# One load per chunk, an opening without holds, and five changes of order in a retention and feed-forward kernel

## The chip, the cores and the metric

The kernel runs on one core of a Trainium2 chip. The metric is the time of one execution on the device, in microseconds (us). Before the change three runs took 639.9, 640.38 and 642.58 us; the median is 640.38. The profiled run took 638.22 us, of which the profile covers a span of 636.4 us.

The engines are named as the profile names them: PE (TensorE matrix products), PEld (its weight loads), DVE (VectorE), ACT (ScalarE), POOL (GpSimd) and SP (SyncE, which issues all the transfers).

## The reference

Two blocks follow each other: a retention layer, computed as a recurrence over 768 tokens for 4 sequences of 8 heads, and a feed-forward block with an ELU on its 3072 tokens.

```python
batch, n_heads, seq, head_dim = (4, 8, 768, 64)
n_tokens, d_model, d_ff = (3072, 512, 2048)

gamma = 1.0 - 2.0 ** (-5.0 - np.arange(H, dtype=np.float32))
scale = 1.0 / np.sqrt(D)
for t in range(S):
    state = gamma[None, :, None, None] * state + np.einsum('bhd,bhe->bhde', k[:, :, t], v[:, :, t])
    y[:, :, t] = scale * np.einsum('bhd,bhde->bhe', q[:, :, t], state)
# x: (B,H,S,D) -> (B*S, H*D)
h = x @ w_in
g = np.where(h > 0.0, h, alpha * (np.exp(np.minimum(h, 0.0)) - 1.0))
return (g @ w_out).astype(np.float32)
```

All inputs of the retention are fp32; the two weight matrices arrive as fp64.

## The kernel before

**Tiling.** The 3072 tokens are cut into 24 chunks of 128, and four chunks make a token block of 512, so there are six blocks (numbered 0 to 5). A chunk has one row of 2048 fp32 numbers for each of the 128 partitions: q and k turned (the tile `qk`, columns 0 to 1023) and k and v plain (the tile `kvn`, columns 1024 to 2047). `load_one` (L106) loads one of the two tiles in a transfer of 512 KB, and `load` (L99) both. Retention within a chunk goes over half chunks of 64 tokens: `score_products` (L308) multiplies q and k, `scores` or `mask_pair` mask the result on DVE, `scale_v` (L281) multiplies v by the powers of gamma (DVE for chunks 0 and 1, POOL for the others), `state_products` (L338) and `state_sum` (L349) make the running states, and `within` (L395) and `across` (L405) add up y. Two small DVE copies called `seen` (L384, L432) stand between the first and the second half of `across`. The scaled y becomes x, the input of the feed-forward block, in the tiles `xb` and `xt`.

**Weights.** They come as 16 pieces of fp64 bits, 1 MB each (`load_piece_parts`, L134), into three staging tiles, and are turned into fp32 by ACT (`prepare`, L151: L168, L170, L172) and DVE (`decode`, L184: L194, L195, L198). At the end of its decoding a piece asks for the next load, since its staging tile is then free. Pieces 0 to 7 are w_in (`w_a`, `w_b`), pieces 8 to 15 are w_out (`w_s` as a first stop).

**Products.** Block 0 uses plain products for the first matrix (`plain_first`, L495) and seven products for four (Strassen's scheme) for the second. Later blocks use the scheme once or twice nested. Its combined weights are made by `combine_w_out`, `combine_w_in` and, on POOL, `combine_small` (L816: four differences and sums of 128x512 at L821, the result written to DRAM). From block 1 on the weights of the second matrix are read back from DRAM in pieces of 256 KB (`wq`) through a ring of 11 tiles (`fetch_small`, L797); the first 11 fetches stand behind the last `combine_small` write on SP.

**Order.** All of it is written out by hand: each engine executes its instructions in the order in which the code emits them, and generators interleave the parts. Four places matter for the change. (1) The opening, L257 to L267 and L1106 to L1167: transfers are issued in the order in which the code wants them, and some are held back by `hold` (L116), a one-element POOL copy from an earlier tile into the new one, so that the new transfer can be issued only after the earlier one has landed. (2) The loop at L1278, which computes the first product of block 1 with `sides` (making combined weights on DVE) and `smalls` (`combine_small` on POOL, for j = 3 after its third turn and j = 2 after its fourth). (3) `second_twice` (L935), the second matrix of a block in products j = 1, 2, 6, 7, 5, 3, 4, each again in seven small products; it yields at points where retention steps of the next block are put in (`VISITS`, L1313: five visits in block 1). In it `copy` (L961, ACT) and `add` (L966, DVE) take the results out of PSUM. (4) `first_end` (L921), which ends a quarter of the first matrix with its ELU (`elu`, L478: ACT L483 and L484, and a DVE instruction L487 that may wait in the list `later`) and, for C22, makes the differences T3 and T1 (L930, L931).

Of the kernel before, what the change touches and what calls it, by code (L numbers as in the profile page):

```python
# [9 lines left out]
FP32 = mybir.dt.float32  # L10
# [8 lines left out]
def kernel(  # L19
# [76 lines left out]
    chunks = [divmod(m, NCH) for m in range(NCHUNK)]  # L96
    raw = {}

    def load(m):  # L99

        if m >= NCHUNK:
            return
        for which in range(2):
            load_one(m, which)

    def load_one(m, which, behind=None):  # L106
        if which == 0:
            raw[m] = [ldpool.tile([P, 2, HP, C], FP32, name="qk", tag="qk"), None]
            t = raw[m][0].rearrange("p a h c -> p (a h c)")
        else:  # L110
            raw[m][1] = ldpool.tile([C, 2, H, D], FP32, name="kvn", tag="kvn")
            t = raw[m][1].rearrange("p a h c -> p (a h c)")
        hold(t, behind)
        nc.sync.dma_start(t, qkv[m, :, 1024 * which : 1024 * which + 1024])

    def hold(t, other):  # L116

# [136 lines left out]

    powers_of(slice(0, 2 * C))

    load(0)  # L257
    parts = load_piece_parts(2)
    next(parts)
    for which in range(2):  # L260
        load_one(1, which, raw[0][which][:, 0, 0])
    next(parts, None)
    pieces = lambda n: staged[n][:, :, 0].bitcast(FP32)
    load_piece(pieces(0))
    load(2)
    load(3)
    load_piece(pieces(1))  # L267

# [542 lines left out]

    W_IN = {2: w_a_[:, :, :, 1], 3: w_s_[:, :, 2]}

    def combine_small(j):  # L816

        t = stage.tile([P, 4, 4, P], FP32, name="wi", tag="stage")
        a11, a12, a21, a22 = (W_IN[j][:, 2 * r : 2 * r + 2, :, c, :] for r in range(2) for c in range(2))
        s1, s2, s3, s4 = (t[:, k].rearrange("p (n f) c -> p n f c", f=2) for k in range(4))  # L820
        tt = lambda o, x, y, op: nc.gpsimd.tensor_tensor(out=o, in0=x, in1=y, op=op)  # L821
        tt(s1, a21, a22, ALU.add)
        tt(s2, s1, a11, ALU.subtract)
        tt(s3, a11, a21, ALU.subtract)
        tt(s4, a12, s2, ALU.subtract)
        to_send.append((scratch3[j - 1], t.rearrange("p k f d -> p (k f d)")))
# [94 lines left out]
    def first_end(n, name, ps, x=None):  # L921

        g = gq[name][:, 2 * n : 2 * n + 2, :]
        nc.vector.tensor_tensor(out=g, in0=ps, in1=g if x is None else x, op=ALU.add)  # L924
        g = g.rearrange("p a b -> p (a b)")

        def combine():
            mine = lambda x: gq[x][:, 2 * n : 2 * n + 2, :].rearrange("p a b -> p (a b)")
            sub = lambda o, x, y: nc.vector.tensor_tensor(out=o, in0=x, in1=y, op=ALU.subtract)
            sub(mine("T3"), mine("C22"), mine("C12"))  # L930
            sub(mine("T1"), mine("C12"), mine("C11"))  # L931

        return lambda: elu(g, g, 3, combine if name == "C22" else None)

    def second_twice(tb, behind_last):  # L935
# [121 lines left out]
        for at, j in enumerate(ORDER2):  # L1057
            last = j == 4 and tb == NTB - 1
            cur = (inner_end if last else inner)(j)
            next(cur)  # L1060
            if j == 1:
                yield "tail"
            for _ in before:
                pass
            if j == 2:
                flush()
                next_input(2)
            if j == 5:
                next_input(6)
            if j == 1:  # L1070

                next(cur)
                yield "elu"
                next(cur)
            parts = input_parts(ORDER2[at + 1]) if at + 1 < 7 else iter(())
            if j in (2, 5):

                next(parts)
            else:
                for _ in parts:  # L1080
                    pass
            if at == 6:
                behind_last()
            if j != 1:
                next(cur)
                yield "middle"
                next(cur)
            for _ in parts:
                pass
            before = cur  # L1090
            yield j
# [28 lines left out]
    y = outputs_of_first()  # L1120
    next(y)
    next(y)
    score_products(sc, 0, 0, 1)
    state_sum(kvs, 0, 0, 0, 1)
    prepare(2, between=lambda: powers_of(slice(2 * C, S)))
    piece = decode(True)
    take()
    take()
    mask_pair(sc, 1)
    scale_v(1)  # L1130
    unread(1, TB)
    inner = plain_first()
    next(inner)
    state_products(kvs, 0, 0, 1, range(2))
# [19 lines left out]
    states(0, 1)  # L1154
    take()
    prepare(2)
    piece = decode()
    take()
    next(inner)
    y = outputs(0, 1)  # L1160
    next(y)
    next(y)
    next(y, None)
    next(inner)
    take()
    take()
    prepare()  # L1167
# [106 lines left out]
    sides = [  # L1274
        itertools.chain(combine_w_in(1), last), itertools.chain(combine_w_in(2), combine_w_in(3)), iter(()), iter(()),
    ]
    smalls = [], [], [3], [2]
    for n in range(NQ):  # L1278
        load(2 * CPB + n)
        cur = first(n)  # L1280
        for at in range(3):
            next(cur)

        for _ in tail:
            pass
        for s in cur:
            next(sides[n], None)
            next(sides[n], None)
            if s == "gap":
                break  # L1290
        for _ in sides[n]:
            pass
        tail = cur
        for j in smalls[n]:
            combine_small(j)
        send_small()
    for m in range(2 * CPB, 3 * CPB):
        scale_v(m)
# [7 lines left out]
    sec = second_twice(1, combine_x_twice)  # L1306
    for _ in range(3):
        next(sec)
    for _ in tail:
        pass  # L1310
    flush()
    next(sec)
    step, VISITS = 0, [(0, False), (2, True), (2, False), (4, False), (5, False)]  # L1313
    for s in sec:
        if s == "middle":
            step += 1
        at = (step, s == "middle")
        if at in VISITS:
            retention_step(2, VISITS.index(at))
        if s == ORDER2[-1]:  # L1320
            break
# [3 lines left out]
    for tb in range(2, NTB):  # L1325
        more = tb + 1 < NTB
        qa, qd, u2, end = {}, {}, {}, None

        def rest(n, j):
            if j == 1:  # L1330
                qa[n] = ps_r.tile([P, 2, TH], FP32, name="qa", tag="r") if n == 0 else bank("a")
            if j == 7:
                qd[n] = ps_r.tile([P, 2, TH], FP32, name="qd", tag="r") if n == 3 else bank("bd"[n % 2])
            first_rest(n, j, qa[n] if j in (1, 6, 5) else qd[n])

        def bring(n):
            if more:
                load((tb + 1) * CPB + n)
                scale_v((tb + 1) * CPB + n)

        def pop(count=1):
            for _ in range(count):
                if later:
                    later.pop(0)()

        bring(0)
        rest(0, 1)
        for _ in tail:
            pass
        tail, parts = iter(()), combine_x_parts()  # L1350
        for at, j in enumerate(TWICE):
            cur = first_twice(tb, j)

            next(cur)
            next(tail, None)
            next(parts, None)
            next(cur)
            for _ in tail:
                pass
            next(parts, None)  # L1360
            if at == 1:

                first_end(0, "C11", qa[0])()
                bring(1)
            next(cur)
            tail = cur
        next(tail)
        bring(2)

        sec = second_twice(tb, combine_x_twice if more else lambda: None)  # L1370
        for n in range(NQ):

            rest(n, 6)
            u2[n] = kept(qa[n])
            if n == 0:
                for _ in tail:
                    pass
            if end:
                end()
            pop()  # L1380
            rest(n, 7)
            m7 = kept(qd[n])
            pop(2)
            if n == 2 and more:
                retention_step(tb + 1, 1)
            if n == 3:
                next(sec)
            rest(n, 5)
            end = first_end(n, "C12", qa[n])
            other = first_end(n, "C22", qa[n], m7)  # L1390
            if n < 3:
                end()
                other()
                rest(n + 1, 1)
                first_end(n + 1, "C11", qa[n + 1])()
                rest(n, 4)
# [12 lines left out]
        next(sec)  # L1409
        end()  # L1410
        flush()
        step = 0
        for s in sec:

            if s == "middle":
                step += 1
            elif step in (1, 4, 5):
                retention_step(tb + 1, {1: 2, 4: 3, 5: 4}[step])
            if s == ORDER2[-1]:
                break  # L1420
        tail = sec
# [51 lines left out]
```

## Time and profile before

| what | value |
|---|---|
| median of three runs | 640.38 us |
| span of the profile | 636.4 us |
| PE busy, whole span | 627.1 us |
| DVE, ACT, POOL busy | 482.6, 253.6, 40.0 us |
| bytes moved | 136.86 MB, mean 215 GB/s |
| PE busy from 0 to 31.2 us | 27.2 us (with idle products that only keep it running) |
| PE busy from 239.0 to 440.0 us | 200.96 of 201.0 us |
| issues of `qk` and `kvn` on SP | 24 and 24, 512 KB each, 6.9 and 7.2 us to landing |
| issues of `wraw` (weights) | 15 of 1 MB, 7.0 us to landing |

The page lists each engine's busy time, then slices of the span, the transfers, the chain of work that ended last, and the costliest groups of instructions. A busy PE is not PE at its peak, since the ends of products are modelled. The views of waits say which instruction waited for whom; "issue" is a wait for nothing that the profile shows. The timeline gives start, length, engine, line and tiles of the instructions in order of time.

The block loop from block 2 on takes 100.4 us for a block. In the first 31 us PE has little to do: the retention of block 0 and the first weights have to arrive first. From 15 to 25 us the transfers run at 413 to 421 GB/s, from 5 to 10 us at 329 GB/s and from 10 to 15 us at 369 GB/s.

### The profile page before, as it was taken

The page shows a single profiled execution, that of the slowest core. Times are in us where ns is not written, and L with a number is a line of the kernel's source. Part 1 is how long each engine was busy: PE and PEld are TensorE (multiplying, and loading weights), DVE is VectorE, ACT ScalarE, POOL GpSimd, SP SyncE. Part 2 cuts the span into 40 slices and gives each one's busy share as a digit, 9 for nine tenths or more (in the row PEclk, how much of TensorE's full clock was granted, in tenths as well). Part 3 has the DMA queues.
Part 4 walks back from the last instruction along what each step waited for, and adds up shares of the span by engine and source line. Part 5 has one row for each costly group of instructions (what it writes and reads, how often), then busy time and mean ns, then how long its engine had stood idle before and what let it go on. Part 6 is the DMA issues. An engine that isn't in the chain of part 4 may idle for free.

```text
span 636.4 us, 16203 instructions
## 1 busy us (share of the span) xinstructions
PE 627.1 (99%) x6680; PEld 561.0 (88%) x6680; DVE 482.6 (76%) x870; ACT 253.6 (40%) x472; POOL 40.0 (6%) x42
## 2 busy tenths in 40 slices
PE   8999999999999999999999999999999999999998
PEld 5764568888889899889999989999988999988997
DVE  5769979978979585589776588867488868557976
ACT  6599735014541113555112556111455311356311
POOL 1112000000810000200000100000110000000000
PEclk9999999999999999999999999999999999999999
DMA  8799867688477688604889802788830788600794
GB/s 301 298 343 356 262 207 211 199 237 254 159 267 248 199 259 285 244 2 120 265 281 312 298 5 53 246 283 270 306 120 2 212 292 262 226 21 2 223 308 165
DMA packets 79210, 136.86 MB, mean 215 GB/s; under 512 B 6688, under 2 KB 32160, under 8 KB 76960
## 3 DMA queue, kind: packets, MB, share of 16 engines
q1 hardware_dynamic: 79136, 135.82, 65.0%
q8 instruction: 53, 0.87, 0.5%
q14 instruction: 21, 0.17, 0.1%
HBM read 114.56 MB, written 21.23 MB: 213 GB/s over the span
## 4 chain that ended last, share of the span: by engine, by line
PE 89%; DMA 5%; DVE 2%; POOL 2%; issue 1%; ACT 1%; SPq 0%; POOLq 0%; DVEq 0%; ACTq 0%
PE pa L955 20%; PE pa L916 10%; PE pd L955 9%; PE pb L955 5%; PE pa L870 5%; PE pb L916 4%; DMA wraw<-in_w_dram 4%; PE pa L527 3%; PE qa L916 3%; PE x L617 3%; PE pd L870 2%; PE qd L916 2%; PE pa L617 2%; PE pd L916 2%; PE y L400 2%; PE y L415 2%
## 5 line engine op out<-in xcount | busy, mean ns | idle before, releaser
L963 ACT COPY ms<-pa 128x128 f32<-128x128 f32 x104 | 27.8, 267 | 147.1 <-PE pa L955 147.1
L955 PE MATMUL pa<-ts,wq 128*128 128x128 f32 x560 | 74.2, 275 | 0.3 <-ACT ms L963 0.3
L955 PE MATMUL pd<-ts,wq 128*128 128x128 f32 x552 | 73.1, 275 | 0.0
L955 PEld LDWEIGHTS pa<-ts,wq 128*128 128x128 f32 x560 | 68.5, 192 | 0.8 <-ACT ms L963 0.5
L955 PEld LDWEIGHTS pd<-ts,wq 128*128 128x128 f32 x552 | 67.1, 192 | 0.3 <-DVE res L967 0.2
L955 PE MATMUL pa<-gC,wq 128*128 128x128 f32 x480 | 64.7, 278 | 0.5 <-DMA wq<-scratch_dram 0.5
L484 ACT ACTIVATE r<-r 128x512 f32<-128x512 f32 x96 | 60.7, 632 | 3.0
L955 PEld LDWEIGHTS pa<-gC,wq 128*128 128x128 f32 x480 | 59.0, 192 | 2.1 <-issue 0.9
L483 ACT ACTIVATE r<-gC 128x512 f32<-128x512 f32 x64 | 40.0, 626 | 32.5 <-DVE gC L924 32.5
L967 DVE TENSOR_TENSOR res<-pd,ms 128x128 f32<-128x128 f32 x68 | 19.6, 288 | 39.8 <-PE pd L955 38.6
L287 POOL TENSOR_TENSOR kvn<-kvn,vf 128x512 f32<-128x512 f32 x22 | 25.8, 1176 | 316.2 <-DMA kvn<-in_qkv_dram 122.2
L487 DVE SCALAR_TENSOR_TENSOR gC<-r,gC 128x512 f32<-128x512 f32 x64 | 43.9, 718 | 0.7 <-ACT r L484 0.7
L832 DVE TENSOR_TENSOR ts<-gC,ts 128x512 f32<-128x512 f32 x60 | 41.3, 689 | 1.0
L832 DVE TENSOR_TENSOR ts<-gC 128x512 f32<-128x512 f32 x60 | 41.1, 685 | 0.0
L955 PE MATMUL pb<-gC,wq 128*128 128x128 f32 x240 | 32.8, 277 | 0.1
L988 ACT COPY res<-pa 128x128 f32<-128x128 f32 x34 | 9.1, 267 | 56.1 <-PE pa L955 54.6
L955 PEld LDWEIGHTS pb<-gC,wq 128*128 128x128 f32 x240 | 29.5, 192 | 0.8 <-DVE gC L487 0.8
L696 ACT COPY m<-pa 128x512 f32<-128x512 f32 x24 | 13.9, 581 | 30.1 <-PE pa L916 13.8
L924 DVE TENSOR_TENSOR gC<-qa,gC 128x512 f32<-128x512 f32 x8 | 5.5, 692 | 25.0 <-PE qa L916 18.3
L916 PE MATMUL pa<-xt,w_s 128*128 128x256 f32 x96 | 23.0, 382 | 0.0
L916 PE MATMUL pa<-xt,w_b 128*128 128x256 f32 x96 | 23.0, 382 | 0.0
L916 PE MATMUL pa<-xb,w_a 128*128 128x256 f32 x96 | 22.7, 379 | 0.0
(257 smaller groups left out, 1258.4 us busy)
## 6 DMA issues: line engine op xcount, KB each, us to landing
wq<-scratch_dram SPq DMA_DIRECT2D x277, 256.0 KB, 4.4
wraw<-in_w_dram SPq DMA_DIRECT2D x15, 1024.0 KB, 7.0
qk<-in_qkv_dram SPq DMA_DIRECT2D x24, 512.0 KB, 6.9
kvn<-in_qkv_dram SPq DMA_DIRECT2D x24, 512.0 KB, 7.2
out_dram<-res SPq DMA_DIRECT2D x14, 256.0 KB, 4.0
scratch_dram<-gT SPq DMA_DIRECT2D x12, 256.0 KB, 4.0
scratch_dram<-m SPq DMA_DIRECT2D x12, 192.0 KB, 4.4
scratch_dram<-so SPq DMA_DIRECT2D x4, 512.0 KB, 4.6
```

What stands on the lines that cost most here:

```text
L287: eng.tensor_tensor(out=kv[:, 1], in0=kv[:, 1], in1=vf[:, i].unsqueeze(2).to_broadcast([C, H, D]), op=ALU.mult)
L483: nc.scalar.activation(e, h, AF.Relu, scale=-1.0)
L484: nc.scalar.activation(e, e, AF.Exp, scale=-1.0)
L487: nc.vector.scalar_tensor_tensor(g, e, -1.0, h, ALU.add, ALU.max)
L527: nc.tensor.matmul(hp, lhsT=w[n][:, fi, j // 2, j % 2, :], rhs=xb[:, j, :], start=(j == 0), stop=(j == 3))
L617: nc.tensor.matmul(X[j][:, d, :], lhsT=w[j][:, d * P : d * P + P], rhs=x[j], start=(n == 0 and d == 0), stop=at_end, skip_group_check=True,)
L832: sub = lambda o, x, y: nc.vector.tensor_tensor(out=o, in0=x, in1=y, op=ALU.subtract)
L870: nc.tensor.matmul(ps[:, f, :], lhsT=lhs[f], rhs=xs[j][k], start=(begin and f == 0), stop=True, skip_group_check=True,)
L916: nc.tensor.matmul(ps[:, fi, :], lhsT=w[:, fi, j2, :], rhs=x[:, j2, :], start=(j in (1, 7) and fi == 0 and j2 == 0), stop=(j2 == 1), skip_ ...
L955: nc.tensor.matmul(ps, lhsT=w[:, f, :], rhs=ts[j][k][:, f, :], start=(begin and f == 0), stop=(f == 3), skip_group_check=True,)
L963: nc.scalar.copy(m, ps)
L967: nc.vector.tensor_tensor(out=o, in0=x, in1=y, op=ALU.add)
```

## The change

The change has two sides, the loads and the order.

Loads: `qk` and `kvn` become one tile `chunk` and one transfer of 1 MB. Only chunk 0 is still loaded in two transfers. In the opening the holds on chunk 1 and on weight piece 1 are gone, so that the transfers are issued in a row; piece 2 is still held behind piece 1. This is for the opening's transfers to follow each other without a pause and for fewer issues.

Order: (a) in the opening an idle product (`unread`) and the scaling of v of chunk 1 move ahead of the scores and masks of chunk 1, and the decoding of piece 2 is cut in two so that the `seen` copies come between its two instructions. (b) `combine_small(2)` is emitted after the first turn of the loop at L1278 rather than after the fourth, with a hold behind `w_s[1]`. (c) At the start of the second matrix of block 1 two steps of the old product's tail and one step of the new one come before the rest of the tail; in the order of the engines this moves one ACT copy `ms` ahead of two ELU instructions. (d) `second_twice` yields "first" after the first step of each product but the first, and the third retention step of block 2 is put there, in product j = 7, which is four small products later than before. (e) In the last of the four quarters the difference T1 is put into the list `later`, so that it comes behind the L487 of C21. The numbers of all instructions on PE, DVE and ACT stay the same; POOL has two holds fewer (three go, one comes), SP has 23 transfers fewer.

```diff
-    def load(m):
+    def load(m, parts=1):
         if m >= NCHUNK:
             return
-        for which in range(2):
-            load_one(m, which)
-
-    def load_one(m, which, behind=None):
...
-        hold(t, behind)
-        nc.sync.dma_start(t, qkv[m, :, 1024 * which : 1024 * which + 1024])
+        t = ldpool.tile([P, 2048], FP32, name="chunk", tag="chunk")
+        raw[m] = (
+            t[:, 0:1024].rearrange("p (a h c) -> p a h c", a=2, c=C),
+            t[:, 1024:2048].rearrange("p (a h d) -> p a h d", a=2, d=D),
+        )
+        for part in range(parts):
+            c = slice(part * 2048 // parts, (part + 1) * 2048 // parts)
+            nc.sync.dma_start(t[:, c], qkv[m, :, c])
...
-    load(0)
+    load(0, 2)
     parts = load_piece_parts(2)
     next(parts)
-    for which in range(2):
-        load_one(1, which, raw[0][which][:, 0, 0])
+    load(1)
     next(parts, None)
-    pieces = lambda n: staged[n][:, :, 0].bitcast(FP32)
-    load_piece(pieces(0))
+    load_piece()
     load(2)
     load(3)
-    load_piece(pieces(1))
+    load_piece(staged[1][:, :, 0].bitcast(FP32))
...
-    def combine_small(j):
+    def combine_small(j, behind=None):
         t = stage.tile([P, 4, 4, P], FP32, name="wi", tag="stage")
+        hold(t.rearrange("p k f d -> p (k f d)"), behind)
...
             sub(mine("T3"), mine("C22"), mine("C12"))
-            sub(mine("T1"), mine("C12"), mine("C11"))
+            if n < NQ - 1:
+                sub(mine("T1"), mine("C12"), mine("C11"))
+            else:
+                later.append(lambda: sub(mine("T1"), mine("C12"), mine("C11")))
...
             for _ in before:
                 pass
+            if at:
+                yield "first"
...
+    unread(1, TB)
     score_products(sc, 0, 0, 1)
...
+    scale_v(1)
     mask_pair(sc, 1)
-    scale_v(1)
-    unread(1, TB)
...
-    piece = decode()
+    piece = decode(True)
     take()
     next(inner)
     y = outputs(0, 1)
     next(y)
     next(y)
+    take()
     next(y, None)
     next(inner)
+    take()
...
-    smalls = [], [], [3], [2]
+    smalls = [2], [], [3], []
...
-            combine_small(j)
+            combine_small(j, w_s[1].rearrange("p s a b c -> p (s a b c)") if j == 2 else None)
...
+    next(tail)
+    next(tail)
+    next(sec)
     for _ in tail:
         pass
     flush()
-    next(sec)
-    step, VISITS = 0, [(0, False), (2, True), (2, False), (4, False), (5, False)]
+    step, VISITS = 0, [(0, "end"), (2, "middle"), (3, "first"), (4, "end"), (5, "end")]
     for s in sec:
-        if s == "middle":
+        if s == "first":
             step += 1
-        at = (step, s == "middle")
+        at = (step, s if s in ("first", "middle") else "end")
```

In the block loop the count of steps moves to "first" in the same way; the order of the instructions there stays as it was.

More of the change, by code (lines that the diff above doesn't have):

```diff
@@ L97 @@
     raw = {}
-    def load(m):
+    def load(m, parts=1):
         if m >= NCHUNK:
             return
-        for which in range(2):
-            load_one(m, which)
-    def load_one(m, which, behind=None):
[L107 to L112, printed above, removed]
-        hold(t, behind)
-        nc.sync.dma_start(t, qkv[m, :, 1024 * which : 1024 * which + 1024])
+        t = ldpool.tile([P, 2048], FP32, name="chunk", tag="chunk")
[6 more added lines that the diff above has]
+            nc.sync.dma_start(t[:, c], qkv[m, :, c])
     def hold(t, other):
@@ L1413 @@
         for s in sec:
-            if s == "middle":
+            if s == "first":
                 step += 1
-            elif step in (1, 4, 5):
+            elif s != "middle" and step in (1, 4, 5):
                 retention_step(tb + 1, {1: 2, 4: 3, 5: 4}[step])
```

## The prediction

> **What bounds the kernel now.** I read the page first, then the chain that ended last from its start, the waits of TensorE (PE) and its weight loads (PEld), and the timeline around each wait.
>
> ```profile
> PE 627.1 (99%) x6680; PEld 561.0 (88%) x6680; DVE 482.6 (76%) x870; ACT 253.6 (40%) x472; POOL 40.0 (6%) x42
> ```
>
> PE carries the span. From 31.2 us on it has almost no hole, so no transfer or vector work counts there unless PE waits for it. The opening differs. Its chain, from 0 to 31 us (start, length, what):
>
> ```profile
> 1.65 5.73 DMA wraw<-in_w_dram
> ...
> 7.43 0.18 POOL wraw L119
> ...
> 7.63 8.06 DMA wraw<-in_w_dram
> ...
> 15.82 0.18 POOL wraw L119
> ...
> 16.02 8.80 DMA wraw<-in_w_dram
> ...
> 27.44 0.69 DVE w_a L198
> 28.13 0.16 DVE seen L384 x2
> ...
> 28.34 0.69 PE y L415 x32
> 29.03 0.84 PE hp L503 x3
> 29.87 0.27 issue
> ```
>
> Weight pieces arrive one after another, two of them issued by a GpSimd (POOL) copy that waits for the previous one. Piece 2 lands at 24.82; its decoding (L198) stands on VectorE (DVE) ahead of the two `seen` copies that release y. What PE still waits for, later included (total us, times, longest):
>
> ```profile
> PE kv L344 <- POOL kvn L287: 0.8, 1, 0.8
> PE y L415 <- issue: 0.8, 1, 0.8
> PE pa L955 <- DMA wq<-scratch_dram: 0.5, 1, 0.5
> PE pa L955 <- ACT ms L963: 0.3, 1, 0.3
> ```
>
> ```profile
> PEld pb L955 <- DVE gC L487: 0.8, 4, 0.2
> ```
>
> The timeline (start, length, instruction) shows the last one:
>
> ```profile
> 593.69 0.69 DVE L929 TENSOR_TENSOR gC<-gC,gC 128x512 f32<-128x512 f32 x1
> 594.30 0.68 DVE L487 SCALAR_TENSOR_TENSOR gC<-r,gC 128x512 f32<-128x512 f32 x1
> 594.41 1.34 PE L955 MATMUL pb<-gC,wq 128*128 128x128 f32 x8
> ```
>
> The T1 difference (second L929) runs ahead of the L487 that finishes C21, and the pb product that reads C21 takes 1.34 us where the others take 1.06.
>
> [...] the first three 512 KB transfers, issued in a row, land at 4.92, 6.17 and 7.43, 1.25 us apart, not together:
>
> ```profile
> 4.92 0.17 POOL L119 COPY qk<-qk 1x1 f32<-1x1 f32 x1 [2.65 <-DMA qk<-in_qkv_dram]
> 6.17 0.18 POOL L119 COPY kvn<-kvn 1x1 f32<-1x1 f32 x1 [1.07 <-DMA kvn<-in_qkv_dram]
> 7.43 0.17 POOL L119 COPY wraw<-wraw 1x1 f32<-1x1 f32 x1 [1.09 <-DMA wraw<-in_w_dram]
> ```
>
> [...] the 128x1024 L198 takes 0.69 us, but 1.46 beside POOL's scaling of v (1.04 us at 19.93). [...]
>
> **The change, part by part.**
>
> *Opening transfers.* Chunks 1, 2, 3 become one 1 MB transfer each and the holds on chunk 1 and piece 1 go; the order on the queue stays chunk 0, half of piece 0, chunk 1, other half, piece 1, chunks 2 and 3, piece 2 (still held behind piece 1). So only gaps can be won. With no gap, the 5.5 MB after 7.4 would take 11 x 1.25 = 13.8 us and piece 2 land at 21.2 instead of 24.82: 3.6 at most. By stretches of 1 us, the transfers ran at 406 to 446 GB/s from 15 to 24, but at 213 to 340 from 7 to 12. Five us at some 295 instead of 415 GB/s lose 5 x 120/415 = 1.4 us. The rest of the 3.6 lies in the slowest of the 16 engines, for which every transfer has to wait: the landing records of v of chunk 2 run from 16.75 on the first engine to 19.79 on the last, and the holds were long over then. I take 1.0, between 0.3 and 2.5.
>
> *Order around it.* Today v of chunk 1 is scaled at 11.97, just as it lands; qk came at 9.8. In one transfer the scores wait for both halves, about 1 to 1.5 us longer, but an idle product is moved ahead of them and the scaling ahead of the masks, so this chain ends within 0.4 us of today's: zero. POOL's scalings of chunks 2 and 3 start earlier [...]: cost 0 to 1, against the 0.8 us PE wait for POOL at 23.5, which goes. I set these equal. Behind piece 2, moving `seen` ahead of L198 lets y (0.69) and its 0.16 run beside the decode, and the 0.27 issue pause need not recur: 0.8. Opening: 1.0 + 0.8 = 1.8 us (0 to 2.9). What follows, 31 to 64 us, is tight on ScalarE (21.8 of 23 us busy from 40 to 63, with waits for weights of 0.7 in all), but those transfers and preparations are released by the same decodings and products, so they move along.
>
> *combine_small(2) first.* Four POOL instructions (6.3 us with DVE beside them, 166.88 to 173.2) move from before the ring's first fetch to near 142. The hold queues them, and on SP the write of their result and chunks 9 and 10, behind w_s[1] (DVE L680, done at 142.3 to 143). Today that write starts at 173.21, lasts 5.5, the fetch follows at 178.82 and PE waits 0.54 at 181.63. Afterwards the last write starts near 167, so the wait goes: 0.55 (0.5 to 0.7). Cost: each POOL instruction stretches a DVE instruction by about 0.9 (L758 1.68 instead of 0.69), 3.6 in all; DVE waits 1.66 + 0.76 + 0.35 us at 145.3, 150.5 and 151.6, and w_s[2] is ready at 157.1 for a product at 159.99. Hidden. Chunks 9 and 10 left at 149 to 151 and are needed at 190: hidden too.
>
> *Tail ahead of the ELU.* At 189.37 PE waits 0.32 for an ACT copy (ms) behind two ELU instructions of 0.63; it now stands before them. 0.4 with the pipeline's refill (0.3 to 0.5).
>
> *y of block 2 later.* That y block runs from 207.70 to 210.72, 3.02 us; its sister at 223.42 to 224.98 takes 1.56. The difference is the issue wait (0.79) and the dribble behind L356, plus 0.24 wait ahead. Four products later (3.6 us) L356 has ended (209.45). 1.4 (0.7 if the issue pause comes along, 1.7 at most).
>
> *T1 after C21.* 1.34 - 1.06 = 0.28, four times: 1.1. The T1 input is read two vector inputs later: hidden.
>
> *One transfer per chunk later on.* Twenty-three fewer issues of 0.4 us on SP, which spends most of its time waiting; the halves of a chunk now land together, in 7 us, some 30 ahead of use. Only chunk 7 is close: it lands at 60.5 and its scores come at 62. Nothing.
>
> Sum: 1.8 + 0.55 + 0.4 + 1.4 + 1.1 = 5.25.
>
> **The rivals.** *A, the opening gives nothing:* DVE is the opening's second chain (from 15 to 21.5 it decodes nearly without pause), [...] the issue pause follows y. Then 0 + 0.55 + 0.4 + 0.7 + 1.1 = 2.75: 640.4 - 2.75 = 637.6. For it: DVE's density and the 1.46 row. Against: the chain of waits names piece 2, not DVE. *B, slower:* without holds the transfers share the engines instead of queueing. Chunk 1, half and whole pieces, chunks 2 and 3 (4.5 MB after 7.4) then all end near 7.4 + 9 x 1.25 = 18.7; chunk 1, due at 11.9, is 6.8 late, and the opening loses 6.5 of it: 640.4 + 6.5 - 2.75 = 644.1. Against it: the 1.25 us spacing above. *C, all gaps close:* 2.9 + 0.7 + 0.5 + 1.7 + 1.1 = 6.9: 633.5. Against: the slowest engine's lag.
>
> **How the numbers follow.** The median of before, 640.38, less 5.25 is 635.1. Chances: forecast 0.55, C 0.15, A 0.22, B 0.08. The bound of 0.5% is 3.2 us, so 637.2. Forecast and C lie below it, and A does not: faster 0.70, same 0.23, slower 0.07 (B's lighter forms are within the bound). The range runs from C, 633.2 with measuring spread, over A to 639.2.
>
> **What would show it.** Piece 2's first preparation (L168) starts near 23.8 instead of 24.91, and the phase of full products near 29.4 instead of 31.2; the scores of chunk 1 come near 11. No PE wait for wq near 180, none for ms, a y block of 1.6 us, pb products of 1.06 after 290, periods of 100.1 instead of 100.4 us. Wrong if piece 2 lands later than 24.8, if L198 rows of 1.4 us multiply before 22 us, or if PE waits for w_s near 158.

## The result

Timed beside the kernel before on one chip, the changed kernel took 635.16 us (median of 4 executions) against 640.79; the ratio is 0.9912, with a 95% interval of 0.9887 to 0.9937. The forecast was 635.1. Two later comparisons of the same two kernels (the runs after_again and after_third below) gave ratios of 0.9934 (0.9911 to 0.9957) and 0.9965 (0.9949 to 0.9981). The third interval doesn't touch the first. Over all three, the medians are 636.46 us (27 executions) and 639.77 (99): 3.3 us less, 0.5%. So the change is faster, but the 5.6 us of the first comparison were its best showing, and the sum of the prediction, 5.25, was too large. That 635.16 met the forecast of 635.1 so closely is luck.

### The profile page after: what moved, and what is told of

It reads as the page before. It is cut to its first block, busy times and chain, and to the rows that moved or that the text cites. A ratio compares the mean times of both kernels' runs of the same rounds, so it can differ in the third digit from the quotient of the medians.

```text
span 634.4 us, 16149 instructions
## 1 busy us (share of the span) xinstructions
PE 626.7 (99%) x6680; PEld 560.7 (88%) x6680; DVE 481.7 (76%) x870; ACT 252.9 (40%) x472; POOL 40.6 (6%) x40
## 4 chain that ended last, share of the span: by engine, by line
PE 94%; DVE 4%; issue 1%; ACT 0%; DVEq 0%
PE pa L953 20%; PE pa L911 10%; PE pd L953 10%; PE pb L953 5%; PE pa L865 5%; PE pb L911 4%; PE pa L521 3%; PE qa L911 3%; PE x L611 3%; PE pa L740 2%; PE pd L865 2%; PE qd L911 2%; PE pd L911 2%; PE pa L611 2%; PE y L394 2%; PE kv L338 2%
## 5 line engine op out<-in xcount | busy, mean ns | idle before, releaser
L965 DVE TENSOR_TENSOR res<-pd,ms 128x128 f32<-128x128 f32 x68 | 19.4, 286 | 39.6 <-PE pd L953 38.4
L281 POOL TENSOR_TENSOR chunk<-chunk,vf 128x512 f32<-128x512 f32 x22 | 26.3, 1199 | 318.4 <-DMA chunk<-in_qkv_dram 153.5
L481 DVE SCALAR_TENSOR_TENSOR gC<-r,gC 128x512 f32<-128x512 f32 x64 | 44.3, 724 | 0.7 <-ACT r L478 0.7
L965 DVE TENSOR_TENSOR res<-res 128x512 f32<-128x512 f32 (+1 forms) x31 | 20.6, 666 | 3.0 <-DVE res L965 0.5
```

Of the source, the lines that this page charges most:

```text
L281: eng.tensor_tensor(out=kv[:, 1], in0=kv[:, 1], in1=vf[:, i].unsqueeze(2).to_broadcast([C, H, D]), op=ALU.mult)
L481: nc.vector.scalar_tensor_tensor(g, e, -1.0, h, ALU.add, ALU.max)
L965: nc.vector.tensor_tensor(out=o, in0=x, in1=y, op=ALU.add)
```

## The profile after

The engine shares, from the page:

```profile
PE 626.7 (99%) x6680; PEld 560.7 (88%) x6680; DVE 481.7 (76%) x870; ACT 252.9 (40%) x472; POOL 40.6 (6%) x40
```

PE has as much work as before and less idle time. The chain from 0 to 32 us (start, length, what):

```profile
18.43 1.32 DVE w_b L194
19.79 1.99 PE pb L497 x8
21.79 1.09 PE sc L307 x64
...
25.73 1.29 PE y L394 x63
...
27.51 0.26 DVE seen L378 x2
27.81 0.69 PE y L409 x32
28.51 1.31 PE hp L497 x5
```

No transfer is in it any more. Before, three weight transfers carried it to 24.8; now DVE's decoding of w_b (L194, which was L198) and then PE's own work carry it. What PE still waits for (total us, times, longest):

```profile
PE pd L740 <- DVE h L695: 1.2, 2, 0.7
...
PE pb L497 <- DVE w_b L194: 0.5, 1, 0.5
```

The waits for wq, for ms, for POOL's kvn and at the y block of block 2 are gone. The first line is new: PE had no such wait before.

To see where the time went, I numbered the 6,680 matmul records of each trace and compared the start of the nth in both. The lead is how much earlier it starts than in the first trace of before; positions are taken where both have the same order. The columns are those positions, by their time in the first trace of before. "ACT near 63" is the start of ACT's first preparation of the weight piece (w_s) that arrives there. The 1.73 of scale_held at 62 stands just ahead of a wait; behind it the lead is 0.86.

| trace | ACT near 63 | 62 | 84 | 149 | 171 | 191 | 224 | end |
|---|---|---|---|---|---|---|---|---|
| before | 63.05 | 0 | 0 | 0 | 0 | 0 | 0 | 0 |
| before_again | 63.61 | 0.27 | -0.70 | -0.70 | -0.71 | -1.10 | -0.87 | -0.87 |
| changed | 62.20 | 0.53 | 0.41 | 0.41 | -1.21 | 0.16 | 1.93 | 2.12 |
| after_again | 62.49 | 0.99 | 0.92 | 0.92 | -0.69 | 0.67 | 1.75 | 1.91 |
| after_third | 62.94 | 1.15 | 0.08 | 0.07 | -1.54 | -0.17 | 1.60 | 1.77 |
| transfers_only | 62.43 | 0.85 | 0.33 | 0.34 | 0.33 | 0.38 | 0.12 | 0.12 |
| orders_only | 65.19 | 0.45 | -2.13 | -2.13 | -3.74 | -2.38 | -0.61 | -0.18 |
| small_last | 62.97 | 0.83 | 0.02 | 0.02 | 0.02 | 0.72 | 2.49 | 2.65 |
| small_early | 62.49 | 0.27 | 0.15 | 0.15 | 0.15 | 1.51 | 3.28 | 2.58 |
| scale_held | 63.85 | 1.73 | -0.82 | -0.82 | -2.44 | -1.08 | 0.69 | 0.64 |
| early_and_held | 63.73 | 0.56 | -0.38 | -0.38 | -0.38 | 0.98 | 2.75 | 1.15 |
| chunks_early | 62.85 | -0.37 | -1.01 | -1.01 | -2.61 | -1.25 | 0.52 | 1.05 |
| chunks_small | 62.84 | -0.21 | -0.63 | -0.63 | -0.63 | 0.73 | 2.50 | 2.80 |
| chunks_small_held | 62.72 | -0.37 | -0.56 | -0.56 | -0.56 | 0.80 | 2.57 | 3.09 |

Two things stand out in the rows of the changed kernel: between 149 and 171 it loses 1.6 us, each time, and the y block (191 to 224) gives more than forecast.

The loss first. The timeline of the changed kernel (start, length, instruction, and in brackets the idle time ahead of it and who ended it):

```profile
145.63 1.73 POOL L816 TENSOR_TENSOR wi<-w_a 128x512 f32<-128x512 f32 x1
146.14 1.63 DVE L647 TENSOR_TENSOR wi<-w_s 128x384 f32<-128x384 f32 x1
147.31 1.58 POOL L816 TENSOR_TENSOR wi<-w_a,wi 128x512 f32<-128x512 f32 x1
147.81 1.51 DVE L647 TENSOR_TENSOR wi<-wi,w_s 128x384 f32<-128x384 f32 x1
149.24 0.54 DVE L647 TENSOR_TENSOR wi<-w_s 128x384 f32<-128x384 f32 x1
...
152.82 0.68 DVE L695 TENSOR_TENSOR h<-pd,m 128x512 f32<-128x512 f32 x1
153.56 1.99 PE L740 MATMUL pd<-xb,w_s 128*128 128x256 f32 x8 [0.73 <-DVE h L695]
...
166.42 1.99 PE L740 MATMUL pd<-xb,w_s 128*128 128x256 f32 x8 [0.44 <-DVE h L695]
```

combine_small(2) on POOL (L816) stretches two DVE sums (L647) from 0.55 to 1.63 and 1.51 us. DVE comes late to h, the sum that empties the bank pd, and PE can't begin the next product in pd. It happens at 153, and again at 166, where DVE has not caught up. In the kernel before, L653 (now L647) took 0.55 us there, h (L701) came earlier, and PE did not wait:

```profile
146.47 0.55 DVE L653 TENSOR_TENSOR wi<-w_s 128x384 f32<-128x384 f32 x1
...
151.55 0.69 DVE L701 TENSOR_TENSOR h<-pd,m 128x512 f32<-128x512 f32 x1 [0.35 <-PE pd L746]
...
153.08 1.89 PE L746 MATMUL pd<-xb,w_s 128*128 128x256 f32 x8
```

## Experiments

### How far one execution speaks for the kernel

Both kernels unchanged, run again; the changed one once more beside the last group of experiments.

> The kernel before, unchanged, to learn how much one run of it differs from another. Theory 1 (the gain is what the pair of traces shows): this run gives about 638 and the timed ones too, so the 640.4 of earlier was high by chance and the change is worth about 2.1 us. Theory 2 (the kernel before scatters more than the changed one, in a place that the first trace does not show): the times spread from 638 to 642 and the trace, aligned with the first one of before, jumps by 1 to 3 us at one or a few places.

> The changed kernel, unchanged, beside the others on one chip. Theory 1: 635 to 636.3 and a ratio near 0.9967 (2.1 us). Theory 2: 635.2 again with little scatter, and a ratio near 0.991 (5.5 us).

> The changed kernel, unchanged, as the measure for the three others on this chip. Between 635 and 636.5; its last piece of w_out of the first row (prepared by ACT near 63) starts between 62 and 63, and its trace is 0.3 to 1.0 us ahead of the first trace of before at 84 us.

before_again took 639.87 us (20 executions, 638.67 to 642.24), ratio 0.9999 (0.9987 to 1.0011). after_again took 636.36 (8 executions, 635.45 to 638.55), after_third 636.68 (15 executions, 635.26 to 639.55), beside 640.01 and 639.29 for the kernel before; their ratios are given under the result. Theory 2 of the first expectation holds in half: the kernel before scatters, and the second trace of it falls behind the first by 0.97 us between 62 and 84. But the changed kernel scatters in the same place: it loses 0.12, 0.07 and 1.07 us there in its three traces, so after_third's expectation for 84 us (0.3 to 1.0) was missed, at 0.08, and its time lies just above the 635 to 636.5 expected. after_again, with 636.36 and 0.9934, falls between its two theories. The first traced execution of before took 638.22, 1.5 under the median of 639.77. That is why the first pair of traces shows 2.1 us and the times more. Averaged over three traces after and two before, the lead at the end is 1.93 + 0.43 = 2.4 us.

### The transfers alone, the orders alone

transfers_only is the kernel before with the loads of the changed one; `load` itself is changed as in the diff of the change, and the opening so:

```diff
-    load(0)
+    load(0, 2)
     parts = load_piece_parts(2)
     next(parts)
-    for which in range(2):
-        load_one(1, which, raw[0][which][:, 0, 0])
+    load(1)
     next(parts, None)
-    load_piece(pieces(0))
+    load_piece()
     load(2)
     load(3)
-    load_piece(pieces(1))
+    load_piece(staged[1][:, :, 0].bitcast(FP32))
```

orders_only is the changed kernel with this turned round.

> The kernel before with only the loads of the changed one: each chunk one transfer, no holds on chunk 1 and piece 1; every order as before. By the prediction, the transfers alone bring 1.0 of the opening's 1.8 us, and the phase of full products begins at 30.2 instead of 31.2. By the rival (the decoding on DVE and the scaling on POOL are the bound once piece 2 comes early), DVE L198 of piece 2 still stands ahead of the copies that release y, chunk 1's scaling comes ahead of nothing, and the phase begins between 30.6 and 31.6; the time is within 0.5 us of before.

> The changed kernel with the loads of the kernel before: half chunks, holds on chunk 1 and piece 1; every order as in the changed kernel. By the prediction it loses the 1.0 us of the transfers against the changed kernel (about 636.2). By the rival, piece 2 lands near 24.8 again, but the decoding of piece 2 no longer stands ahead of y, so the loss is 0.3 to 0.8 us only where the weights are waited for at 28.5, and the rest of the gain (about 1.5 us in the trace) remains.

transfers_only: 639.36 us, ratio 1.0001 (0.9979 to 1.0022). orders_only: 638.35, ratio 0.9970 (0.9955 to 0.9986). On the same chip after_again had 0.9934. The transfers alone give nothing that can be measured in the time; on top of the orders they give 2.0 us by the medians (the two intervals just overlap), twice the 1.0 of the prediction and more than the 0.3 to 0.8 of the rival.

In the opening itself the transfers came near the prediction. transfers_only began its full products at 30.37 (30.2 foretold, 30.6 to 31.6 by the rival), where the two traces of before began them at 31.22 and 30.95; orders_only began at 30.77, the changed kernel at 30.56, 30.23 and 30.07. And transfers_only, with the old order, has the decoding of piece 2 (L194, at 26.66 for 0.69 us) done before `seen` (L378) is due, so that `seen` waits for PE alone:

```profile
27.62 0.24 DVE L378 COPY seen<-y 128x8 f32<-128x8 f32 x2 [0.26 <-PE y L409]
```

The traces put the 2.0 us between 62 and 84: at 62 the lead of orders_only is 0.45, of the changed kernel 0.53 to 1.15, but at 84 it is -2.13 against 0.08 to 0.92. What PE waited for in orders_only between 60 and 220 us:

```profile
PE pd L746 <- DVE h L701: 1.2, 2, 0.7
PE kv L344 <- issue: 0.9, 1, 0.9
PE y L400 <- DVE kvn L356: 0.6, 1, 0.6
```

The timeline has ACT's preparation of the weight piece near 63. In the kernel before:

```profile
63.05 1.16 ACT L168 ACTIVATE w_s<-wraw 128x1024 uint32<-128x1024 uint32 x1 [0.52 <-DMA wraw<-in_w_dram]
```

In orders_only:

```profile
65.19 1.14 ACT L168 ACTIVATE w_s<-wraw 128x1024 uint32<-128x1024 uint32 x1 [1.23 <-DMA wraw<-in_w_dram]
```

In after_third, and with it how a late piece reaches PE:

```profile
62.94 1.17 ACT L164 ACTIVATE w_s<-wraw 128x1024 uint32<-128x1024 uint32 x1 [0.45 <-DMA wraw<-in_w_dram]
...
68.90 0.69 DVE L191 TENSOR_SCALAR wraw<-wraw 128x1024 uint32<-128x1024 uint32 x1
...
70.77 0.42 DVE L350 TENSOR_TENSOR chunk<-kv,carry 128x256 f32<-128x256 f32 x1
...
71.79 1.55 PE L394 MATMUL y<-chunk 64*64 64x64 f32 x62 [0.63 <-DVE chunk L350]
```

The decoding (L191 and then L194, at 69.63 for 1.23 us) stands ahead of the state sums (L350) on DVE, and y waits for those. In the table, the lead at 84 is about the smaller of two numbers: the lead at 62, and 63.05 less ACT's start. orders_only: -2.14 foretold, -2.13 seen; after_third 0.11 and 0.08; scale_held, below, -0.80 and -0.82. It fits within 0.5 us in all traces but chunks_early, which lost 1.25 us in one pause at 68. The wait in the profile agrees with it: y near 72 us waits for a sum behind this decoding in before_again, orders_only, after_third, small_last, scale_held and early_and_held (0.28 to 0.63 us), all with ACT's piece after 62.9, and in none with an earlier piece (the first trace of before, at 63.05 and with no lead, has no such wait either). A second cause lies in the same stretch: transfers_only lost its 0.5 in a pause put down to "issue" at 66.8 (0.77 us), and orders_only has one of 0.90 there besides its wait at y. That orders_only falls so far back for want of the merged transfers rests on its one trace and on the medians: the kernel before has the same loads, and its piece came at 63.05 and 63.61.

### combine_small(2) in other places

small_last puts it back, small_early puts it 13 us earlier, where DVE waits for PE and then only adds PSUM to SBUF.

In small_last the hold is left out too:

```diff
-    smalls = [2], [], [3], []
+    smalls = [], [], [3], [2]
...
-            combine_small(j, w_s[1].rearrange("p s a b c -> p (s a b c)") if j == 2 else None)
+            combine_small(j)
```

In small_early the hold is on the third sum of small_of_pieces(3):

```diff
             ms = [ms[:, k, 0:3] for k in range(4)]
+            held["s3"] = ss[:, 2].rearrange("p f c -> p (f c)")
...
             some(held["last"], 3)
+            combine_small(2, held["s3"])
...
-    smalls = [2], [], [3], []
+    smalls = [], [], [3], []
...
-            combine_small(j, w_s[1].rearrange("p s a b c -> p (s a b c)") if j == 2 else None)
+            combine_small(j)
```

> The changed kernel with combine_small(2) back in its old place, after the last quarter, without a hold. By the prediction (the cost of the early place is hidden), the wait for wq near 181 comes back and the time grows by 0.55 us, to 636.9. By the theory from the trace (the early place stretches DVE L647 to 1.6 and 1.5 us, DVE is late by 1.7 us and the two products that reuse the bank pd wait 0.7 and 0.4 us for DVE L695), the two waits at 153 and 166 go, wq comes back, and against the changed kernel's trace it gains 1.0 to 1.6 at 166 and keeps 0.5 to 1.0 after 182: 635.4 to 635.9.

> The changed kernel with combine_small(2) one block earlier: held behind the third sum of small_of_pieces(3) (DVE L647 at 128.3), so that POOL runs from 129 to 134, where DVE idles 2.35 us and then only adds with one operand in PSUM. By the prediction, DVE's lateness was hidden, so nothing changes against the changed kernel (0 within 0.3). By the theory from the trace, no DVE instruction is stretched (L647 0.55, L595 0.69), the waits of pd for DVE h at 153 and 166 go, no wait for wq comes, and it gains 1.2 to 1.7 us in the trace: 634.7 to 635.2.

small_last: 635.51 us, ratio 0.9935 (0.9919 to 0.9951); small_early: 635.28, ratio 0.9934 (0.9919 to 0.9949). small_last lies within the 635.4 to 635.9 of the theory from the trace and not near the 636.9 of the prediction; small_early lies just above the theory's 634.7 to 635.2. The changed kernel was not timed on this chip, so the table of leads decides it: all traces with combine_small(2) at 142 us or just behind lose 1.60 to 1.62 between 149 and 171, and all with it elsewhere 0.00 or 0.01. small_early's POOL and DVE:

```profile
131.00 1.27 POOL L817 TENSOR_TENSOR wi<-wi,w_a 128x512 f32<-128x512 f32 x1
131.60 0.69 DVE L595 TENSOR_TENSOR gT<-x,m 128x512 f32<-128x512 f32 x1 [2.32 <-PE x L611]
132.22 1.27 POOL L817 TENSOR_TENSOR wi<-w_a 128x512 f32<-128x512 f32 x1
132.41 0.69 DVE L595 TENSOR_TENSOR m<-pa,m 128x512 f32<-128x512 f32 x1
...
146.32 0.55 DVE L647 TENSOR_TENSOR wi<-w_s 128x384 f32<-128x384 f32 x1
146.90 0.56 DVE L647 TENSOR_TENSOR wi<-wi,w_s 128x384 f32<-128x384 f32 x1
```

No DVE instruction is stretched: L595, which has one operand in PSUM, kept its 0.69 us beside POOL. The changed kernel's trace has both cases in one instruction, L481, beside combine_small(3):

```profile
162.26 1.27 POOL L816 TENSOR_TENSOR wi<-w_s 128x512 f32<-128x512 f32 x1 [13.36 <-DVE w_s L674]
...
162.70 3.07 DVE L481 SCALAR_TENSOR_TENSOR gC<-r,h 128x512 f32<-128x512 f32 x2
...
163.60 1.61 POOL L816 TENSOR_TENSOR wi<-wi,w_s 128x512 f32<-128x512 f32 x1
...
165.18 1.72 POOL L816 TENSOR_TENSOR wi<-w_s 128x512 f32<-128x512 f32 x1
...
166.29 0.67 DVE L481 SCALAR_TENSOR_TENSOR gC<-r,pa 128x512 f32<-128x512 f32 x1
```

Two with both inputs in SBUF (r, h) take 3.07 us; at 150.77, with POOL idle, one takes 0.67. With one input in PSUM (pa) it takes 0.67 beside POOL too. No run moved an operand alone. In small_last, PE's waits between 140 and 200 us are down to one, the old one:

```profile
PE pa L953 <- DMA wq<-scratch_dram: 0.4, 1, 0.4
```

small_last gains 0.70 from 171 to 191, the changed kernel 1.37 in each of its traces (1.36 to 1.37). So losing the wait for wq is worth 0.67, as the prediction had it (0.55), and its place cost 1.61. small_early has both, 1.36 and no loss, but ends no better than small_last: it lost 1.1 us to a late chunk 1 at 12 us, which the hold can't have caused (POOL runs it at 129), and 0.75 to a pause in the y block near 302:

```profile
302.08 0.34 PE L409 MATMUL y<-chunk 64*64 64x64 f32 x7 [0.54 <-issue]
```

### POOL's scaling held behind the decoding

scale_held lets POOL scale v of chunks 2 and 3 only after the half of w_b that stands at that moment on DVE. early_and_held joins this to small_early.

```diff
-    scale_v(2)
-    scale_v(3)
     prepare(2, by_vector=True)
     next(inner)
     piece = decode()
-    take()
-    take()
+    for m in (2, 3):
+        take()
+        hold(raw[m][1][:, 1].rearrange("p h d -> p (h d)"), w_b[0].rearrange("p a b c d -> p (a b c d)")[:, 512 * m - 1024 :])
+        scale_v(m)
```

> The changed kernel with POOL's scaling of v of chunks 2 and 3 held (by POOL copies) behind the first and second half of w_b on DVE. By the prediction [...], DVE L194 falls from 1.31 to 0.69 us both times. [...] the product pb comes at 19.2 instead of 19.79 and the phase of full products 0.4 to 0.6 us earlier (635.9); if the transfers bound, pb is earlier, but the phase is not (within 0.15 us).

> The two before in one kernel. If the two are independent, the sum: 1.6 to 2.3 us below the changed kernel, 634.1 to 634.8, and 5.2 to 6 us below the kernel before. If the opening's time is given back later, only that of combine_small: 635.

In the changed kernel's opening the first half of w_b (L194) starts at 18.43 and takes 1.31 us:

```profile
18.12 1.07 POOL L281 TENSOR_TENSOR chunk<-chunk,vf 128x512 f32<-128x512 f32 x1 [3.05 <-DMA chunk<-in_qkv_dram]
...
19.79 1.99 PE L497 MATMUL pb<-xb,w_b 128*128 128x256 f32 x8 [0.52 <-DVE w_b L194]
```

In scale_held's opening the two halves start at 17.77 and 19.40 and take 0.69 and 1.31 us:

```profile
18.51 1.59 PEld L497 LDWEIGHTS pb<-xb,w_b 128*128 128x128 f32 x8 [0.31 <-DVE w_b L194]
...
18.92 1.24 POOL L281 TENSOR_TENSOR chunk<-chunk,vf 128x512 f32<-128x512 f32 x1
```

The first L194 falls to 0.69; the second stays at 1.31, which the expectation missed: the held scaling (1.24 us from 18.92) runs beside it. PE comes to pb 1.28 us earlier than in this trace of the changed kernel (0.62 of it is the shorter L194; the rest began ahead of it). after_third is the fairer measure, since its decoding of w_a ahead of this place begins at 15.83 and scale_held's at 15.80: pb comes 0.69 earlier than there, and the lead at 62 is 0.58 larger, within the 0.4 to 0.6 expected. So the stretched first half was on the path. Yet nothing of it lasts: the scores of chunk 7 now come before their chunk,

```profile
61.09 0.69 PE L307 MATMUL sc<-chunk 64*64 64x64 f32 x32 [0.65 <-DMA chunk<-in_qkv_dram]
```

and ACT's piece comes at 63.85: the lead at 84 is -0.82. scale_held took 636.2 us (ratio 0.9954, 0.9944 to 0.9964). early_and_held took 634.51 (ratio 0.9935, 0.9917 to 0.9953); its trace gives back 0.94 us from 62 to 84 and waits for 1.5 in the pause at 303. The times of the two can't tell a sum from combine_small alone.

### Chunks 4 to 7 issued earlier

If the stream of transfers sets the stage to 84, moving 1 MB chunks into the idle time from 28 to 33 should help.

```diff
     states(0, 1)
     take()
+    load(CPB)
...
     next(y, None)
+    load(CPB + 1)
...
-        if n in (0, 2, 4, 6):
-            load(CPB + n // 2)
+        if n in (2, 4):
+            load(CPB + 1 + n // 2)
```

chunks_small adds small_early to it, chunks_small_held both small_early and scale_held.

> The changed kernel with chunks 4 to 7 issued earlier: chunk 4 behind weight piece 4 and chunk 5 behind it, ahead of piece 5 (the transfers stand idle from 28 to 33), chunks 6 and 7 each one weight piece earlier. Nothing else changes. By the theory that the stage from 62 to 84 us is set by when the weight piece that ACT prepares near 63 has landed, and not by the opening: ACT's waits for transfers between 30 and 76 (0.7 to 1.1 us in the changed kernel) go, the piece is prepared 0.5 to 1 us earlier, the 0.2 to 0.6 us that PE loses near 72 and 78 go, and the trace is ahead of before at 84 by as much as at 62 (0.6 to 1.0); the time is 0.3 to 0.8 below the changed kernel and scatters less. By the rival [...], ACT starts earlier but PE does not: within 0.2 us.

> The run before with combine_small(2) near 129 us (held behind the third sum of small_of_pieces(3)). By the sum of the single effects: 1.2 to 1.6 from combine_small, 0.3 to 0.8 from the chunks, so 1.5 to 2.4 below the changed kernel; 0.8 less if the pause in the y block near 302 us, which followed this placement twice, comes again.

> The run before with POOL's scalings of chunks 2 and 3 held behind the decoding of w_b. Alone, this brought PE 1.0 us earlier at 62 us but lost it by 84 to the late weight piece. By the theory of the weight stream, with the chunks out of the way, at least half of it now lasts to the end: 0.4 to 1.0 below the run before. By the rival, it is given back again between 62 and 84: within 0.2.

chunks_early took 637.36 us (ratio 0.9976, 0.9964 to 0.9987), chunks_small 636.10 (0.9948, 0.9929 to 0.9966), chunks_small_held 635.66 (0.9954, 0.9937 to 0.9970); after_third, beside them, 636.68 (0.9965). chunks_early was to be faster and came out slower. The timeline says where. In after_third:

```profile
28.01 2.22 PE L497 MATMUL hp<-xb,w_a 128*128 128x256 f32 x8
```

In chunks_early:

```profile
28.06 1.32 PE L497 MATMUL hp<-xb,w_a 128*128 128x256 f32 x5
30.84 0.81 PE L497 MATMUL hp<-xb,w_a 128*128 128x256 f32 x3 [1.47 <-issue]
```

In the middle of hp, PE stood for 1.47 us with nothing to wait for that the views of waits show (1.7 and 1.6 in the other two; the last section has what ran near it). By the starts of the matmuls it lost 1.63 us there, where the three traces of the changed kernel lose 0.26, 0.53 and 0.26. The same matmuls run in both; the difference is chunk 4's transfer in flight, 0.94 MB from 28 to 31 against 0.02 in after_third. So the test of the stream was spoiled: the lead was lost at 30, not at 62. What remains of it settles nothing: ACT's waits for weights between 30 and 76 were 0.5, 0.8 and 0.7 us, and the loss from 62 to 84 was 0.64, 0.42 and 0.19. That is less than in after_third (2.0 and 1.07), but not less than in the other two traces of the changed kernel (0.7 and 1.1; 0.12 and 0.07). chunks_small came to 0.6 us below after_third, where 1.5 to 2.4 was expected. In chunks_small_held the hold had nothing to win: in chunks_small POOL already missed the first half of w_b (0.69 us), and pb came at 18.67 without the hold and 18.90 with it. So this run can't tell its two theories apart.

No version here is faster than the changed kernel beyond the intervals. By the traces small_last, with 633.9 us, and chunks_small_held, with 633.5, have the shorter spans (after: 634.4, 634.6, 634.8), and moving combine_small(2) is the part that the traces show.

## Why the prediction was right or wrong

The forecast was faster, with 635.1 in a range of 633.2 to 639.2; all three medians of the changed kernel lie in the range. That the first of them met 635.1 is luck, since the terms of the sum come to 2.4 in the traces. About half of the mechanisms held: the waits for wq and ms, the y block, the first half of T1. The opening, "they move along" and "Hidden" did not. Means of three traces after, less means of two before:

| part | predicted | seen |
|---|---|---|
| opening, to 62 us | 1.8 | 0.89 - 0.13 = 0.76 |
| 62 to 84 | 0 | -0.42 + 0.49 = 0.07 |
| place of combine_small(2), 84 to 171 | 0 | -1.61 |
| wait for wq and ms, 171 to 191 | 0.95 | 1.37 + 0.20 = 1.57 |
| y of block 2, 191 to 224 | 1.4 | 1.54 - 0.12 = 1.42 |
| T1 after C21, 224 to the end | 1.1 | 0.17 |
| sum | 5.25 | 2.4 |

**Opening: the term was mis-sized, and three of its steps failed.** Piece 2 was prepared at 22.86 instead of 24.91 (22.69 and 22.79 beside 24.26 in the other traces), nearly twice the 1.0 that I took. But then nobody waited for it. `seen` ahead of the decode worked: DVE ran it at 27.51, L194 at 27.67, and y no longer waits for weights. The full products that I put near 29.4 began at 30.56.

- The sum 1.0 + 0.8 counted one wait twice. Both parts take the decoding of piece 2 out of the way of `seen`; transfers_only had it out of the way with the old order, so the order had little left to win.
- "I set these equal" failed; the cost of 0 to 1 us there was an estimate. PE waits for DVE instead, which the rival A had named. The first half of w_b took 1.31, 1.30 and 1.35 us beside POOL, where it had taken 0.69 in both traces of before. PE waited 0.52 to 0.57 us for it, pb came no earlier than before (19.79, 19.38 and 19.20 against 19.17 and 19.24), and scale_held showed that the first half without POOL beside it (0.69 us) brings PE forward (pb 0.69 earlier than in after_third). The 0.8 us wait for POOL that was to pay for this stood in only one of the two traces of before.
- The issue pause that "need not recur" recurred in all three traces.

**"They move along" failed.** What follows 31 us does not move with the opening. Five traces were ahead by over 0.8 us at 62. In the three with ACT's piece after 62.9 (after_third, small_last, scale_held) the lead was gone at 84; with the piece at 62.43 and 62.49, transfers_only kept 0.33 of it (the rest went in the pause at 66.8) and after_again 0.92. Here the merged transfers seem to count, which I had put at nothing: orders_only, without them, falls to -2.13. Why the piece comes late is open; the last section has what its landings show.

**combine_small(2): "Hidden" failed.** I had summed the stretch of DVE (3.6 us) against its idle time (2.8) and looked only at when w_s[2] is ready. Its consumer did not wait. The bank pd did: its next product needs h read out of it first, and h stands in DVE's order behind the two stretched sums. The gain side, 0.67, was right. Net, this part cost 0.9 us.

**ms: right.** The changed kernel gains 1.37 from 171 to 191 where small_last, still waiting for wq, gains 0.70. Of the latter 0.12 is a shorter wq wait (0.58 lost instead of 0.70), which leaves 0.57 for ms (0.4 predicted, an estimate above the 0.32 us of the wait).

**y of block 2: right, a little small.** The five visits were not tested one by one; the size is read at its place in the trace. In ten of the eleven traces that have the later place, the stretch from 191 to 224 gives exactly 1.77 against the first trace of before (predicted 1.4, 1.7 at most). The block now takes 1.56 us, and the issue pause did not come along:

```profile
210.81 1.16 PE L394 MATMUL y<-chunk 64*64 64x64 f32 x64
...
212.37 1.16 PE L953 MATMUL pa<-ts,wq 128*128 128x128 f32 x8
```

In after_again a pause of 0.56 in a kv block at 205 took 0.7 of it.

**T1: the first half right, the second missed.** The pb product takes 1.06 us, as predicted, and PE gains 0.28 us in each of the four blocks. But the 0.69 us of the difference (L924 at 396.06) only moved behind it on DVE, and three microseconds later a sum (L965) that empties pd is late, which takes 0.16 back each time:

```profile
396.06 0.69 DVE L924 TENSOR_TENSOR gC<-gC,gC 128x512 f32<-128x512 f32 x1
396.19 0.97 PEld L953 LDWEIGHTS pb<-gC,wq 128*128 128x128 f32 x8
...
399.60 0.28 DVE L965 TENSOR_TENSOR res<-pd,ms 128x128 f32<-128x128 f32 x1
...
399.93 0.97 PEld L953 LDWEIGHTS pd<-ts,wq 128*128 128x128 f32 x8
```

That leaves 0.5 of the 1.1, and the period of a block is 100.28 us where I had put 100.1 (100.41 before). It is the same mistake as with combine_small: I asked who reads the delayed result, and not which bank the instructions behind it have to free. The other 0.35 missing from the table is lost once, at 335.70, where a product waits for such a sum again: DVE had stood 0.46 us ahead of a sum at 327.98. orders_only and the three runs with early chunks have the same order and lose nothing there, so this isn't the work of T1; its cause is open.

**What stays open.** The pooled medians differ by 3.3 us, the traces by 2.4. The two traced executions of before (638.22 and 639.16) lie below its median of 639.77, 1.1 on average, and the three after (636.29, 636.50, 636.64) on theirs. That covers the difference in size; which pauses the slower executions of before had, no trace of one shows. Of the five changes of order only the place of combine_small(2) was run apart; the sizes of the others are read from the traces at their places.

## What to carry to other kernels

When a change delays an engine off the critical path, follow everything queued behind the delay, above all the reads that free a PSUM bank for the next product (here PE waited 0.73 and 0.44 us for h). Before two gains are added, ask whether they remove the same wait. A gain in an early stage can be lost in the next one, as here between 62 and 84 us (from 1.15 to 0.08 in after_third); the traces point to a stream of transfers and decodings there that keeps its own time. And try POOL's work with SBUF operands where VectorE reads PSUM: here VectorE's sums with an operand in PSUM kept their 0.69 us beside it (L595), and those of two SBUF operands went from 0.55 to 1.63 and 1.51 (L647).

## What the runs showed of the hardware

**Each longer pause put down to "issue" ends shortly after a packet of the instruction queue, and the longest pauses in hp came with a transfer in flight.** The instruction queue of the profile moves 53 packets of 16 KB in each trace. After the first 15 us, PE has 20 pauses of over 0.15 us put down to "issue" in the fourteen traces together, and each of them ends 1.2 to 1.6 us after one of these packets has ended; at most three of the 53 packets in a trace end in such a pause. In hp, PE lost 0 to 0.84 us in the eleven traces with almost nothing on the DMA engines (at most 0.11 MB from 28 to 31 us), and 1.63, 1.90 and 1.77 us in the three that had a 1 MB transfer running. In those three the packet started 0.3 to 0.8 us behind the first matmul of hp; in the eleven others it started 0.6 to 2.0 us ahead of it. That PE waits for the packet, and that the packet comes late because data is ahead of it, is the author's reading of these times; no run moved the packet alone.

**The slowest of the 16 DMA engines sets the landing, and its lag changes from one execution to the next.** In the kernel before, the 16 landing records of the first transfer run from 4.25 to 4.86 us, and the POOL copy that waits for it starts at 4.92; those of weight piece 2 run from 21.78 to 24.82, and ACT's preparation of it starts at 24.91. By the landing records of the transfers from 36 to 60 us, the time from the first engine's landing to the last one's was on average 0.76 us in the first trace of the changed kernel and 0.75 in the second, but 2.24 in the third, of the same program. It was 2.51 in orders_only, 2.19 in small_last and 2.69 in scale_held, all of which lost 0.8 us or more from 62 to 84; before_again, at 1.97, lost 0.97. early_and_held, at 0.65, lost 0.94 without it, so it isn't the only cause.
